# A sum and difference form for the last two inverse transforms, a third buffer for w2, and a new order from its first third on

## The chip, the cores and the metric

The kernel runs on one core of one Trainium2 chip. A core has five engines, each with a queue of its own that is worked off in order: TensorE (PE in the profile, with its weight loads as PEld) multiplies matrices into accumulators (PSUM), VectorE (DVE) and ScalarE (ACT) work element by element, GpSimd (POOL) does small set-up work and starts the accumulating and the scattering stores, and SyncE (SP) starts nearly all other transfers between HBM and the on-chip memory (SBUF). The metric is the device time of one execution in microseconds (us), as a median of runs.

## What is computed

The reference adds two branches under a gate. S is 2048 tokens, D 640 channels, F 1536.

```
x  = A_q                                            # (1, S, D), bf16
g  = sigmoid((x * gate_w).sum(-1))                  # one gate per token
# branch a: shift by 4 taps, long causal convolution over S, gate by q
kv = (sum over t<4 of k shifted by t * shift_k[:, t]) * v
y  = irfft(rfft(kv padded to 2S) * rfft(ssm_k padded to 2S))[:S]
a  = x * (y + kv * ssm_D)
# branch b: token-mixing MLP on the layer-normed x
u  = gelu(einsum("bsd,sf->bdf", layernorm(x), w1) + b1)
b  = einsum("bdf,fs->bsd", u, w2) + b2
out = g * a + (1 - g) * b
```

## The kernel before

**Branch a.** The 2048 tokens are cut into P = 4 blocks of 512. The convolution is done block by block in a frequency domain of 4 groups of 128 frequencies (`fi` 0 to 3): the filter's blocks go to tables `W0` to `W3`, the blocks j of kv to tiles `A0`, `A1` (a product with cosine and sine tables on TensorE, function `a_freq`), and VectorE forms the products `A[j] * W[m - j]` and adds them up for output block m in a tile `Z` (function `pair`; three real products stand for a complex one). Blocks 0 and 1 of kv are done early, blocks 2 and 3 late. Z of the last block is finished in four pieces, one a frequency group.

**The inverse.** `inverse(m_)` takes Z of output block m_ back to tokens. It makes four results of 128 x 640, P and Q for k = 0 and 1, each the sum of four products of a 128 x 128 table (`TIc`, `TIs` or a negated copy in `TIn`) with Z's four frequency groups. A product is two matmuls, because 640 columns are taken as two halves of 320. For the last block the products are issued frequency by frequency, for the others result by result. ScalarE copies the four results to a tile `pq` (evictions).

**The epilogue.** `epilogue(m_)` takes sums and differences of `pq` into `y` (VectorE), multiplies with `xe`, which is x times the gate, and adds to the output: blocks 0 to 2 by an accumulating store onto rows that the other branch has written, block 3 on chip, one token tile of 128 at a time, with stores of its own.

**Branch b.** After the layer norm, `mlp1` makes u in six steps, and `mlp2(q)`, q = 0 to 7, multiplies it with a block of w2 of 256 tokens (768 KB), loaded by `w2_load` to `w2_0` or `w2_1` in turn. A block is 2 token tiles of 12 products of two matmuls. For q of 6 and 7 ScalarE also makes a reversed copy `w2r` of half the block. The result of token tile 14 stays in its accumulator until VectorE adds it in the epilogue of block 3; its column halves are computed one after the other.

**The order.** Building the kernel first lists all operations (`_Plan.add`, numbered as they are created), with what each must wait for, worked out from the overlap of the memory that they touch. `_Plan.run` then issues them in the order of the list `ORDER`, which is written out in the file, and each engine's queue, SyncE's and GpSimd's included, has its operations in that order. Four accumulators of 128 x 1280 are handed out in turn as `ORDER` goes. The addresses of all SBUF tiles are written out in `OFFS`; tiles that are not needed at the same time share addresses. Matmuls are issued in line 311, ScalarE's operations in line 691, VectorE's two-operand ones (`tt`) in line 653, so the profile's groups are told apart by their tiles.

Of the kernel before, what the change touches and what calls it, by code (L numbers as in the profile page):

```python
# [422 lines left out]
def _checked(items, offs, base, top):  # L423
# [49 lines left out]
def _build(nc, A_q, A_k, A_v, A_shift_k, A_ssm_k, A_ssm_D, B_x, B_w1, B_b1, B_w2, B_b2, gate_w, out):  # L473
# [13 lines left out]
    FOLD = (2, 3)  # L487
    NSET = FT // FSET
# [3 lines left out]
    with ExitStack() as es:  # L492
# [62 lines left out]
        buf("TIn", [128, 4, 128], BF16, 45, END)  # L555
        buf("wz", [128, 128], BF16, 0, 8)
# [33 lines left out]
        for i in range(2):  # L590
            buf(f"w2_{i}", [128, FT, 256], BF16, 101, END)
        for i in range(2):
            buf(f"pq{i}", [128, 4, D], BF16, (64, 67)[i], END)
# [10 lines left out]
        for name, shape, dtype, t0, t1 in spec:  # L604
# [263 lines left out]
        iota(b["rev"][:, :], [[256, NT // 2]], 255, -1, 0.4)  # L868

# [341 lines left out]
        def w2_load(q):  # L1211
            nm = f"w2_{q % 2}"
            dma(b[nm][:, :, :], dram(B_w2, q * 256, [[S, 128], [128 * S, FT], [1, 256]]), nm, 40.0 + q)
# [4 lines left out]
        def mlp2(q):  # L1218
            plan.tag = f"m2_{q}"
            w2_load(q)  # L1220
            w2 = b[f"w2_{q % 2}"]
# [33 lines left out]
        def inverse(m_):  # L1255
# [7 lines left out]
            }  # L1263
            pq = b[f"pq{m_ % 2}"]
# [4 lines left out]
            last = m_ == P - 1  # L1269
            if last:  # L1270
                for k in range(2):
                    for fi in ORD:
                        mms = []
                        for w in "PQ":
                            c = 0 if w == "P" else 1
                            mms += halves(res[w, k], [(tabs[w, k][fi], Z[:, c, fi, :])], fi == 0, fi == 3)
                        pe([res["P", k], res["Q", k]], mms, 1.0)
            else:
# [8 lines left out]
            return pq  # L1287

        def epilogue(m_, pq, pr):
            y = b["y"]  # L1290
            t0 = 4 * m_
            o_ = b[f"o{m_ % NO}"]
            xe = b[f"xe{m_ % 2}"]
# [144 lines left out]
```

## Time and profile before

| what | value |
|---|---|
| median of three runs | 190.25 us (190.23, 190.25, 191.79) |
| the profiled execution | 190.98 us, span 189.2 us |
| TensorE busy | 178.8 us, 95% of the span, 1590 matmuls |
| VectorE busy | 175.5 us, 93%, 246 operations |
| ScalarE busy | 125.5 us, 66%, 202 operations |
| GpSimd busy | 35.2 us, 19% |
| transfers | 40.37 MB, mean 213 GB/s |

The span is the time from the first to the last instruction of the program in the profiled execution; what the execution takes beyond it lies around the program. Busy is the time in which an engine had at least one instruction under way. The rows of a time order show start, duration, engine, line, operation, the tile written, the tiles read, and in brackets the idle time before it with what ended it. Consecutive like instructions are merged (x and their count). A row of a group shows line, engine, operation, shapes, count, then busy time and mean duration in ns of one, then idle time before. Instructions of an engine overlap in the records: one starts before the one before it has been written out, so the distance between starts is shorter than a duration. A row by stretch shows the stretch, its length, the busy time and count of PE, PEld, DVE, ACT and POOL, the granted clock of TensorE, the share of the transfer engines and GB/s.

### The profile page before, as it was taken

To read this page: it belongs to the slowest core of one execution; us is meant where nothing else is said; L and a number is where in the kernel's file an instruction comes from. 1 tells how busy PE (TensorE), PEld (TensorE's weight loads), DVE (VectorE), ACT (ScalarE), POOL (GpSimd) and SP (SyncE) were. 2 spreads that over 40 slices of the span, in tenths; PEclk is the share of its full clock that TensorE was granted. 3 is DMA by queue.
4 is the path that set the end of the run, shared out by engine and by line. 5 is a ranking of instruction groups with operands and counts; after the bars stand their busy time and mean duration, and the time that the engine had idled before them with its cause. 6 is when DMAs were issued, how large, how long until landed. Compare 5 with 4: busy or idle time off the path is not lost.

```text
span 189.2 us, 3940 instructions
## 1 busy us (share of the span) xinstructions
PE 178.8 (95%) x1590; PEld 123.0 (65%) x1590; DVE 175.5 (93%) x246; ACT 125.5 (66%) x202; POOL 35.2 (19%) x68
## 2 busy tenths in 40 slices
PE   7778899999999999999999999999999899999992
PEld 2345666566667757777767777777667577777771
DVE  7999999999999999999899999999999999997352
ACT  4978999787699489439823047706778482495930
POOL 8366076610000000101000000000005003110732
PEclk9999999999999999999999999999999999999999
DMA  5999999798996876787948998997988976979992
GB/s 155 315 325 272 130 152 282 221 222 190 236 326 129 196 202 181 151 248 164 232 67 221 231 243 197 219 242 205 309 280 224 225 226 221 232 215 240 175 166 69
DMA packets 81094, 40.37 MB, mean 213 GB/s; under 512 B 40051, under 2 KB 80884, under 8 KB 81076
## 3 DMA queue, kind: packets, MB, share of 16 engines
q1 hardware_dynamic: 78340, 37.18, 78.5%
q0 software_dynamic: 2736, 2.95, 9.3%
q8 instruction: 12, 0.20, 0.4%
q14 instruction: 6, 0.05, 0.1%
HBM read 26.03 MB, written 7.54 MB: 177 GB/s over the span
## 4 chain that ended last, share of the span: by engine, by line
PE 61%; DVE 22%; ACT 4%; issue 4%; DMA 4%; POOL 2%; POOLq 1%; DVEq 0%
PE pp L311 61%; DVE stats L919 6%; DMA w<-in_B_w_dram 4%; DVE v L653 3%; DVE en L653 3%; DVE es L653 2%; DVE idx L660 2%; DVE W L653 2%; ACT pq L691 1%; POOL rstd L924 1%; ACT xe L691 1%; DVE h L661 1%; DVE eo L1006 1%; DVE mv L921 1%; DVE A L653 1%
## 5 line engine op out<-in xcount | busy, mean ns | idle before, releaser
L311 PE MATMUL pp<-h,w 128*128 128x320 bf16 x384 | 57.1, 299 | 0.2
L311 PE MATMUL pp<-gT,w 128*128 128x320 bf16 x336 | 48.4, 299 | 0.9 <-DMA w<-in_B_w_dram 0.9
L311 PEld LDWEIGHTS pp<-h,w 128*128 128x128 bf16 x384 | 36.8, 98 | 15.9 <-issue 1.8
L311 PEld LDWEIGHTS pp<-gT,w 128*128 128x128 bf16 x336 | 32.6, 98 | 14.0 <-DMA w<-in_B_w_dram 1.4
L653 DVE TENSOR_TENSOR tt<-A,W 128x3840 bf16<-128x3840 bf16 (+2 forms) x16 | 27.8, 1738 | 0.3
L691 ACT ACTIVATE A<-pp 128x640 bf16<-128x640 f32 x32 | 21.3, 700 | 9.3 <-PE pp L311 9.3
L653 DVE TENSOR_TENSOR Z<-Z,tt 128x3840 bf16<-128x3840 bf16 (+1 forms) x14 | 26.2, 1868 | 0.2
L262 POOL DMA_DIRECT2D out_dram<-xe x3 | 3.8, 1252 | 73.0 <-DVE Z L653 68.4
L691 ACT ACTIVATE o<-pp,c,omg 128x640 bf16<-128x640 f32 x13 | 11.2, 881 | 6.8 <-PE pp L311 6.4
L691 ACT ACTIVATE ks<-pp 128x512 bf16<-128x512 f32 (+1 forms) x24 | 11.1, 518 | 6.1 <-PE pp L311 6.1
L691 ACT ACTIVATE gT<-pp,bf 128x640 bf16<-128x640 f32 x12 | 9.4, 792 | 8.2 <-PE pp L311 8.1
L691 ACT ACTIVATE xe<-xe,gg 128x640 bf16<-128x640 bf16 x16 | 12.7, 827 | 2.4 <-DMA xe<-rows_q 1.2
L919 DVE BATCH_NORM_STATS2 stats<-x 128x6 f32<-128x320 bf16 x32 | 13.7, 472 | 0.0
L653 DVE TENSOR_TENSOR Z<-A,W 128x3840 bf16<-128x3840 bf16 x6 | 12.8, 2154 | 0.9 <-PE pp L311 0.8
L691 ACT ACTIVATE pq<-pp 128x640 bf16<-128x640 f32 x16 | 10.3, 702 | 4.8 <-PE pp L311 4.8
L671 POOL MEMSET W<- 1x640 bf16 x4 | 2.7, 665 | 50.9 <-ACT nq L691 49.6
L691 ACT ACTIVATE W<-pp 128x640 bf16<-128x640 f32 x18 | 12.0, 722 | 0.1
L653 DVE TENSOR_TENSOR W<-W 128x2560 bf16<-128x2560 bf16 x8 | 11.9, 1486 | 0.0
L653 DVE TENSOR_TENSOR y<-pq 128x1280 bf16<-128x1280 bf16 (+1 forms) x10 | 6.6, 688 | 4.5 <-ACT pq L691 4.5
L311 PE MATMUL pp<-kT,dg 64*64 64x256 bf16 x320 | 10.5, 271 | 0.3 <-ACT Wo L691 0.3
L311 PE MATMUL pp<-eo,TFc 128*128 128x320 bf16 x48 | 8.9, 300 | 1.1 <-ACT TFc L691 1.1
L653 DVE TENSOR_TENSOR Z<-Z 128x1280 bf16<-128x1280 bf16 (+1 forms) x16 | 9.9, 653 | 0.1
(147 smaller groups left out, 303.6 us busy)
## 6 DMA issues: line engine op xcount, KB each, us to landing
w<-in_B_w_dram SPq DMA_DIRECT2D x24, 256.0 KB, 4.1
w<-in_B_w_dram SPq DMA_DIRECT2D x8, 768.0 KB, 5.1
wnat<-in_A_ssm_k_dram SPq DMA_DIRECT2D x4, 640.0 KB, 5.7
x<-in_A_q_dram SPq DMA_DIRECT2D x7, 320.0 KB, 6.3
out_dram<-o SPq DMA_DIRECT2D x6, 320.0 KB, 6.1
v<-in_A_v_dram SPq DMA_DIRECT2D x4, 320.0 KB, 4.5
rows_q<-in_A_q_dram SPq DMA_DIRECT2D x8, 160.0 KB, 3.2
xe<-in_A_q_dram SPq DMA_DIRECT2D x4, 320.0 KB, 5.8
```

What stands on the lines that cost most here:

```text
L262: ins = engobj.dma_start(out_ap, in_ap, accum_op=ALU.add)
L311: ins = self.nc.tensor.matmul(ps_ap, lhsT=lhsT, rhs=rhs, start=start, stop=stop)
L653: return vop(eng, c, lambda e: e.tensor_tensor(out_, in0, in1, op), [in0, in1], [out_], pr, kind="tt")
L660: return e.tensor_scalar(out_, in0, s1, None, op0=op0)
L661: return e.tensor_scalar(out_, in0, s1, s2, op0=op0, op1=op1)
L671: return vop(eng, 0.03 + nel(ap) / 1200.0, lambda e: e.memset(ap, val), [], [ap], pr, kind="ms")
L691: return e.activation(out_, src, func, **kw)
L919: vop("DVE", 0.393, (lambda o_, i_: lambda e: e.bn_stats(o_, i_))(o_, i_), [i_], [o_], pr, kind="bn")
L921: vop("DVE", 0.11, (lambda o_, i_: lambda e: e.bn_aggr(o_, i_))(o_, i_), [i_], [o_], pr, kind="ba")
L924: vop("POOL", 0.7, (lambda o_, i_, e_: lambda e: e.tensor_tensor(o_, i_, e_, ALU.pow))(b["rstd"][:, sl], b["vpe"][:, sl], bc(c_mh, [[8, 12 ...
L1006: vop("DVE", 0.74, lambda e: e.tensor_copy(dst, src()), [src], [dst], 0.3, ps=[p_], kind="ev")
```

## The change

Three things are changed.

1. For blocks 2 and 3 (`UV`), the inverse makes other results. The tables are such that, for k = 0 and k = 1, frequency groups 0 and 1 enter a pair of results with different tables, while groups 2 and 3 enter with the same table up to a sign. A new table `TU` (six parts of 128 x 128) holds half the sum and half the difference of `TIc` and `TIs` for two of the four groups, and a negated copy. With it the four results are the half-sum and half-difference of the former P's and of the former Q's, and in each of the four one product is empty (`None`): three products stay of four. After the evictions VectorE takes the sum and the difference of these, for P and Q at once (two `tt` over 2 x 640 elements a partition), into `y`; these are the former four results. `epilogue` then works with `pq` and `y` exchanged. `TU` is made by two `tt` on VectorE and two scalings on ScalarE (`tu_make`).
2. w2 gets a third buffer, `w2_2`, at an address that a tile of w1 and one of kv's tiles used before; the blocks q = 0 to 7 go to buffers 0, 1, 0, 1, 2, 0, 1, 2.
3. `ORDER` is new from its entry 404 on. Operations created behind `tu_make` have numbers 4 higher, those behind inverse(2) 6 and those behind inverse(3) 8 higher, so the entries before that differ in the list are in part the same operations. Among other things the new order puts block 3's kv products on VectorE earlier, the loads of w2's blocks 4 to 7 earlier, the first tile of w2's block 6 ahead of inverse(3), the four evictions of inverse(3) ahead of the last reversed copy of w2, and the products of token tile 15 ahead of all but the first of tile 14's.

```
@@ ORDER: 861 entries for 853 @@
...
-    384, 377, 400, 274, 407, 540, 385, 361, 401, 417, 542, 541, 436, 544, 273, 435, 282, 359, 448, 437, 360, 546, 449, 416,
+    385, 377, 545, 553, 384, 281, 400, 359, 282, 544, 401, 361, 546, 436, 435, 547, 416, 437, 548, 274, 407, 555, 454, 438,
...
+    UV = (2, 3)
...
+        buf("TU", [128, 6, 128], BF16, 101, END)
...
+        buf("w2_2", [128, FT, 256], BF16, 120, END)
...
-            "ncol": 211776, "A0": 211840, "TIs": 227200, "b2x": 228224, "wz": 228288, "gz": 228544,
+            "ncol": 211776, "A0": 211840, "TIs": 227200, "b2x": 228224, "TU": 100224, "w2_2": 182912, "wz": 228288, "gz": 228544,
...
+        def tu_make():
+            plan.tag = "tu"
+            TU = b["TU"]
+            tt(TU[:, 0:2, :], TIc[:, 2:4, :], TIs[:, 2:4, :], ALU.add, 30.0)
+            tt(TU[:, 2:4, :], TIc[:, 2:4, :], TIs[:, 2:4, :], ALU.subtract, 30.0)
+            act(TU[:, 0:4, :], TU[:, 0:4, :], ACT.Copy, 30.0, scale=0.5)
+            act(TU[:, 4:6, :], TU[:, 2:4, :], ACT.Copy, 30.0, scale=-1.0)
...
-            nm = f"w2_{q % 2}"
+            nm = f"w2_{(0, 1, 0, 1, 2, 0, 1, 2)[q]}"
...
+            if m_ in UV:
+                TU = b["TU"]
+                tabs = {
+                    ("P", 0): [TU[:, 0, :], TU[:, 3, :], None, ti(TIc, 3)],
+                    ("Q", 0): [TU[:, 0, :], TU[:, 5, :], ti(TIs, 2), None],
+                    ("P", 1): [TU[:, 2, :], TU[:, 1, :], ti(TIc, 2), None],
+                    ("Q", 1): [TU[:, 4, :], TU[:, 1, :], None, ti(TIs, 3)],
+                }
...
+            for k in range(2):
+                fis = {w: [fi for fi in ORD if tabs[w, k][fi] is not None] for w in "PQ"}
+                def part(w, sel):
+                    c = 0 if w == "P" else 1
+                    return halves(res[w, k], [(tabs[w, k][fi], Z[:, c, fi, :]) for fi in sel],
+                                  sel[0] == fis[w][0], sel[-1] == fis[w][-1])
+                if m_ == P - 1:
                     for fi in ORD:
+                        ws = [w for w in "PQ" if fi in fis[w]]
+                        pe([res[w, k] for w in ws], [m for w in ws for m in part(w, [fi])], 1.0)
+                else:
                     for w in "PQ":
+                        pe([res[w, k]], part(w, fis[w]), 1.0)
...
-            return pq
+            if m_ not in UV:
+                return pq, b["y"]
+            y = b["y"]
+            tt(y[:, 0:3:2, :], pq[:, 0:3:2, :], pq[:, 1:4:2, :], ALU.add, 50.0)
+            tt(y[:, 1:4:2, :], pq[:, 0:3:2, :], pq[:, 1:4:2, :], ALU.subtract, 50.0)
+            return y, pq
...
         def epilogue(m_, pq, pr):
-            y = b["y"]
+            pq, y = pq
...
+        tu_make()
         kv_two(2)
```

More of the change, by code (lines that the diff above doesn't have):

```diff
@@ L1220, in mlp2 @@
             w2_load(q)
-            w2 = b[f"w2_{q % 2}"]
+            w2 = b[f"w2_{(0, 1, 0, 1, 2, 0, 1, 2)[q]}"]
             o_ = b[f"o{(q // 2) % NO}"]
@@ L1268, in inverse @@
                     res[w, k] = _PS()
-            last = m_ == P - 1
-            if last:
-                for k in range(2):
-                    for fi in ORD:
[L1273 to L1278, printed above, removed]
-                for k in range(2):
+            for k in range(2):
[5 more added lines that the diff above has]
+                if m_ == P - 1:
+                    for fi in ORD:
+                        ws = [w for w in "PQ" if fi in fis[w]]
+                        pe([res[w, k] for w in ws], [m for w in ws for m in part(w, [fi])], 1.0)
+                else:
                     for w in "PQ":
-                        c = 0 if w == "P" else 1
-                        pe([res[w, k]], halves(res[w, k], [(tabs[w, k][fi], Z[:, c, fi, :]) for fi in ORD]), 1.0)
+                        pe([res[w, k]], part(w, fis[w]), 1.0)
             for k in range(2):
```

42 rows, old and new, of the table ORDER are left out of this document.

## The prediction

> **What bounds the kernel now.** I read the page's shares and its chain of waits first, then that chain in order of time, then the engines by stage.
>
> ```profile
> span 189.2 us, 3940 instructions
> PE 178.8 (95%) x1590; PEld 123.0 (65%) x1590; DVE 175.5 (93%) x246; ACT 125.5 (66%) x202; POOL 35.2 (19%) x68
> PE 61%; DVE 22%; ACT 4%; issue 4%; DMA 4%; POOL 2%; POOLq 1%; DVEq 0%
> ```
> ```profile
> 49.74 92.22 PE pp L311 x858
> 141.96 6.96 DMA w<-in_B_w_dram
> ```
> ```profile
> 100.00:142.00 42.00, 42.00 (x413) 30.43 (x402) 41.65 (x31) 21.51 (x39) 0.00 (x0) 1.00 0.96 238
> 149.00:170.00 21.00, 21.00 (x155) 15.08 (x156) 20.57 (x26) 12.02 (x17) 2.58 (x3) 1.00 0.85 215
> 170.00:185.60 15.60, 15.54 (x115) 10.96 (x112) 8.46 (x16) 9.66 (x13) 5.54 (x6) 1.00 0.87 181
> ```
>
> TensorE holds most of the chain (61%): it carries it alone from 49.74 for 92 us. Its busy time equals the stretch in the first two rows and misses it by 0.06 in the third, and the granted clock is 1.00 in each. The one hole is the weight tile `w` of the second token matmul. VectorE is just as full, but only up to 170: in 170 to 185.6 it is busy for 8.46 us of 15.6. ScalarE has room everywhere. So two engines stand side by side until Z of the last block is done, and then TensorE alone has work that waits for nobody: the second token matmul. The matmuls of the last stage, in order of time:
>
> ```profile
> 146.82 1.25 PE L311 MATMUL pp<-gT,w 128*128 128x320 bf16 x8
> 148.96 2.35 PE L311 MATMUL pp<-gT,w 128*128 128x320 bf16 x16 [0.89 <-DMA w<-in_B_w_dram]
> 154.95 9.94 PE L311 MATMUL pp<-gT,w 128*128 128x320 bf16 x72
> 183.75 1.79 PE L311 MATMUL pp<-gT,w 128*128 128x320 bf16 x12
> ```
>
> The hole is 0.89 us. The 72 matmuls take 9.94 us, and a matmul by itself 0.30 (the 299 ns of the groups below), so one comes every 9.64/71 = 0.136 us. The last ends at 183.75 + 1.79 = 185.54. VectorE's end, and what follows it:
>
> ```profile
> 167.72 2.09 DVE L653 TENSOR_TENSOR Z<-Z 128x640 bf16<-128x640 bf16 x5
> 170.43 1.56 DVE L653 TENSOR_TENSOR y<-pq 128x1280 bf16<-128x1280 bf16 x2 [0.62 <-ACT pq L691]
> 173.87 0.49 DVE L653 TENSOR_TENSOR y<-pq 128x640 bf16<-128x640 bf16 x1 [0.35 <-ACT pq L691]
> 177.92 1.29 DVE L653 TENSOR_TENSOR y<-pq 128x640 bf16<-128x640 bf16 x3 [3.56 <-ACT pq L691]
> 184.87 0.49 DVE L653 TENSOR_TENSOR xe<-xe,o 128x640 bf16<-128x640 bf16 x1 [2.52 <-ACT o L691]
> 185.27 1.01 DVE L1327 SCALAR_TENSOR_TENSOR xe<-pp,omg,xe 128x320 bf16<-128x320 f32 x2
> ```
> ```profile
> 176.58 1.30 ACT L691 ACTIVATE pq<-pp 128x640 bf16<-128x640 f32 x2
> 183.95 0.88 ACT L691 ACTIVATE o<-pp,c2x,omx 128x640 bf16<-128x640 f32 x1 [2.92 <-PE pp L311]
> 182.37 4.31 SPq L265 DMA_DIRECT2D out_dram<-xe  x3
> ```
>
> Z of block 3 is whole at 169.81. After that VectorE waits for ScalarE's evictions four times. The last two operations, which add the matmul result of token tile 14, end at 186.28; the last store is issued up to 186.68, and the span ends at 189.2, so 2.92 us lie behind VectorE's last operation. The profiled execution took 190.98, which is 1.78 more than its span; the median of the three runs is 190.25. I work against the span and take the difference off the median, since two of the three runs are at 190.23 and 190.25.
>
> **The change, part by part.**
>
> *Fewer matmuls.* Blocks 2 and 3 have four results each, each a sum of four products; of every result one product goes. Two column halves make that 4 x 2 = 8 matmuls a block.
>
> ```profile
> L311 PE MATMUL pp<-Z,TIs 128*128 128x320 bf16 x36 | 7.3, 299 | 0.0
> L311 PE MATMUL pp<-Z,TIc 128*128 128x320 bf16 x36 | 7.2, 299 | 0.0
> L311 PE MATMUL pp<-Z,TIn 128*128 128x320 bf16 x24 | 5.4, 299 | 0.0
> ```
>
> These rows are the inverse of blocks 1 to 3: 96 matmuls, 32 a block, so 24 stay in each of two. Sixteen at 0.136 us are 2.18 us, on an engine without holes. Their weight loads (98 ns each) run beside matmuls and add nothing. The Trainium skill, page "TensorE: Matmul & The Clock Gate", section "Back-to-back issue gap", speaks against the size of this: it gives 81 ns a matmul at 128 columns and 131 at 512 in a stream of loads and matmuls, by which 320 columns would be near 106 ns (an estimate between its two figures), sixteen of them 1.7 us, and the forecast 0.5 us later. The trace's 136 ns decides.
>
> *The third w2 buffer.* Today the load of w2's block 4 goes to the buffer of block 2 and cannot start before that is read.
>
> ```profile
> 141.96 0.60 SPq L265 DMA_DIRECT2D w<-in_B_w_dram  x1
> DMA to landing us min/median/max: 3.2/5.0/7.0
> ```
>
> It is issued at 141.96 and lands 6.96 us later (the chain's row), the longest of the tile's 3.2 to 7.0. In the new list it stands at place 649 instead of 686, behind block 2's load and six loads of `xe`. Block 2's load waits for block 0's last product, which by the new order ends near 127; seven issues of 0.4 to 1.2 us put block 4's at about 132, landing by 139 even with 7 us. Its first matmul moves forward too: 296 matmuls from there to the end are 40.2 us, so it comes about 142.3. The margin is 3 us, and the 0.89 us go. Blocks 5 to 7 get their buffers earlier for the same reason.
>
> *What VectorE gets.* Four passes over 1,280 elements (sum and difference, two blocks) and two of 256 for the table `TU`.
>
> ```profile
> 130.26 0.82 DVE L653 TENSOR_TENSOR y<-pq 128x1280 bf16<-128x1280 bf16 x1
> 131.00 2.15 DVE L653 TENSOR_TENSOR tt<-A,W 128x3840 bf16<-128x3840 bf16 x1
> L653 DVE TENSOR_TENSOR v<-es 128x1280 bf16<-128x1280 bf16 x8 | 6.4, 818 | 0.0
> L653 DVE TENSOR_TENSOR c<-omg,bf 128x16 f32<-128x16 f32 x1 | 0.2, 167 | 0.0
> ```
>
> A pass of 1,280 starts 0.74 us before the next operation. The new ones take every second row of a tile; half of the passes `v<-es` read so too, and last 0.82 like the others. Writing every second row is not shown; split into two passes of 640 (0.49 us each with 0.08 overlapped, the row at 173.87) one would cost 0.82, so it is 0.74 to 0.82, and I take 0.74: four are 2.96 us. A 256-element pass lies between 0.17 (16 elements, the last row) and 0.49 (640); I take 0.2, two make 0.4. In all 3.36 us on the full engine. What of it counts: the table's 0.4 us falls ahead of Z3's end. The first difference of block 2 is queued ahead of the last subtraction of Z3, another 0.74. All of Z3 but that subtraction (0.41) is then ready at 169.81 + 0.4 - 0.41 = 169.8, and its last piece at 169.81 + 0.4 + 0.74 = 170.95. By the new order the earliest matmul that reads a piece made just before 169.8 has 88 matmuls from itself to the end, and the one that reads the last piece has 66; counted back from a TensorE end of 182.5 they start at 170.5 and 173.5. The margins are 0.7 and 2.5 us, and the second token matmul covers the rest. If that cover went, each microsecond past the margin would be one on the end.
>
> *ScalarE* gets two scalings of the table, 512 and 256 elements.
>
> ```profile
> L691 ACT ACTIVATE TIn<-TIs 128x128 bf16<-128x128 bf16 x2 | 0.7, 332 | 0.0
> L691 ACT ACTIVATE w2r<-w 128x1536 bf16<-128x1536 bf16 x2 | 3.0, 1479 | 0.0
> 128.59 0.17 ACT L691 ACTIVATE gth<-pp 128x4 f32<-128x4 f32 x1 [5.62 <-PE pp L311]
> ```
>
> Between 0.33 us (128 elements) and 1.48 (1,536), a straight line gives 0.64 and 0.44, together 1.1. They are queued just after the row at 128.59, ahead of which ScalarE is idle for 5.62 us; inverse(2), which reads the table, comes after the hole at 148.96. Nothing of it counts.
>
> *The tail.* Here a wait is added: the first sum of block 3 reads all four evicted results, where today the pair of k = 1 is enough, and behind it stand every epilogue operation of block 3 and the stores. In exchange the four evictions now stand ahead of the 1.49 us reversal of w2 on ScalarE. The last matmul of inverse(3) has 64 behind it: 182.5 - 8.7 = 173.8. Two evictions lead to 175 at most; sum and difference end at 176.5, eight operations of 0.41 us at 179.8. Then comes the row of tile 15 (today's 184.87), which waits for its eviction: the matmuls of tile 15 end with 20 behind them, 182.5 - 2.7 = 179.75, and today 0.96 us pass from their end (183.91, which is 185.54 less twelve pitches) to 184.87. So it starts at 180.7, with VectorE 0.9 us early. Four operations of 0.41 and the last two (1.01) end at 183.35. From TensorE's side, today's 0.74 us between its end and VectorE's (186.28 - 185.54) give 183.2. Both agree, against 186.28 today.
>
> *The sum.* -2.18 - 0.89 = -3.07 on TensorE (end 182.47), -2.93 at VectorE's last operation, and the same 2.92 behind it: span 186.27, which is 187.3 against the median. Adding up each engine's new order with the starts and durations of the trace, I find about twenty places where ScalarE hands an accumulator to TensorE with less than 0.5 us to spare (nearest at about 117 us). Today such a place looks like this:
>
> ```profile
> 132.03 6.71 PE L311 MATMUL pp<-gT,w 128*128 128x320 bf16 x48
> 138.68 0.30 PE L311 MATMUL pp<-es,AFs 128*128 128x320 bf16 x1
> ```
>
> The last of the 48 starts at 138.44, the next matmul 0.24 later instead of 0.136: 0.10 us lost. I count six of these after 60 us, 0.6 us in all. The new order may lose less (down to none, 0.6 us gained) or more (1 us, if half of the twenty do). I add 0.2: **187.5 us**.
>
> **Rivals.**
>
> *VectorE becomes the bound.* Its margin at Z3 is 0.7 us.
>
> ```profile
> 136.12 1.55 DVE L653 TENSOR_TENSOR v<-kt,v 128x1280 bf16<-128x1280 bf16 x2
> 119.38 3.38 SPq L260 DMA_TRANSPOSE xt<-in_A_q_dram  x1
> v<-in_A_v_dram SPq DMA_DIRECT2D x4, 320.0 KB, 4.5
> ```
>
> The first product of block 3's `v` moves from 136.12 to about 128.4, and its load, behind the transposed load of the second row, which comes a microsecond later, is issued at about 123.5: with the 4.5 us of the last row it lands at 128. For it: no margin there, and a load may take 7 us, as one of `w` did; VectorE is then 2 us late and TensorE 1.3: 188.8. Against: 4.5 is the median of four. It gives 188.0 to 189.3.
>
> *The third buffer does not take the wait away,* or another of its size appears at an earlier `w`: 0.89 back, 188.4. Against it stands the 3 us of margin.
>
> *The transfers back up (slower).* The new list issues from 123.4 to about 133.5 what today is spread up to 142: three blocks of w2 (768 KB), three loads of 320 KB and six of 160, 4.3 MB up to and with w2's block 3, whose first matmul comes at about 143.
>
> ```profile
> 123.00:141.00 18.00, 18.00 (x152) 12.98 (x150) 17.83 (x15) 9.56 (x17) 0.00 (x0) 1.00 1.01 270
> 125.00:130.00 5.00, 5.00 (x55) 3.74 (x54) 4.93 (x3) 1.29 (x4) 0.00 (x0) 1.00 0.79 168
> ```
>
> Today this stretch moves 270 GB/s with the engines' share at 1.01, full. At that rate 4.3 MB take 16 us, landing at 139.4. At 220 GB/s the margin is gone; at 190 the wait is 3 us and the gain is used up (190.3). At the 168 of the second row it is 25.8 us and a wait of 6.2: 193.4. So it decides from 220 GB/s down, and is slower than before below 190. Against it: the low row is a lull with a share of 0.79, not a limit.
>
> *The new order eats the gain* in small waits: the lists agree up to entry 404 of 853, and twenty handovers losing 0.15 us each cost 3 us: 190.3. Against it: today's list has been full over the same stretch, and shows one hole.
>
> **How the numbers follow.** The forecast has 0.62 (187.2 to 187.9). VectorE as the bound 0.13, the wait that stays 0.08, the small waits 0.08, the backed-up transfers 0.09. About 1% either way, 188.35 and 192.15, is what a measurement of this kernel can tell, its three runs being 0.8% apart. Faster by more: the forecast, half of VectorE's case and half of the wait that stays, 0.72. Slower: the transfers' case and 0.01 of the small waits, 0.10. Within: the rest, 0.18. The range goes from 186.6 (today's 0.6 us of late matmuls gone as well, from 187.3) to 189.9, which leaves out the transfers' case and the small waits.
>
> **What would show it.** TensorE: 80 matmuls on `Z`, 8 fewer from each of blocks 2 and 3, its last ending near 182.5, and no hole at a `w` load. The load of block 4 issued near 132. VectorE: four more passes `y<-pq` of 1,280 elements near 0.74 us, and its last operation near 183.35. The store rows as today, 2.9 us behind it. I am wrong if TensorE shows holes after 60 us of over 1 us in sum: ended by `Z` or `es`, VectorE is the bound; by `w`, the transfers; by ScalarE's evictions, the order. If TensorE ends at 182.5 and the span does not follow, the tail's sum was wrong.

## The result

| | before | after |
|---|---|---|
| median of 6 runs each, taken together | 191.05 us (190.23 to 191.88) | 188.41 us (187.38 to 188.71) |
| profiled execution, its span | 190.98, 189.2 | 188.71, 186.9 |

The ratio is **0.9862, with a 95% interval of 0.9827 to 0.9896**: faster by 1.4%. The forecast was 187.5 us for a kernel at 190.25, a ratio of 0.986. The kernel before itself has medians between 190.25 and 191.05 from one set of runs to the next, so only ratios are compared below.

The page of the changed kernel, its size, its engines and the shares of the chain:

```profile
span 186.9 us, 3913 instructions
PE 175.8 (94%) x1574; PEld 121.6 (65%) x1574; DVE 178.9 (96%) x252; ACT 126.9 (68%) x204; POOL 35.3 (19%) x68
PE 56%; DVE 27%; DMA 8%; issue 2%; POOL 2%; SPq 1%; ACT 1%; DVEq 0%; POOLq 0%
```

The lines are those of the changed file, three further on than before (L653 is L656, L691 is L694). VectorE is now busier than TensorE (178.9 against 175.8 us), and 8% of the chain are transfers, where it was 4%. The chain in order of time names two of them:

```profile
102.39 4.41 DMA w<-in_B_w_dram
...
133.57 10.38 DMA w<-in_B_w_dram
144.00 36.61 PE pp L311 x268
```

Two loads of `w`, one of them 10.38 us from its issue to its landing; after it TensorE carries the chain alone. The busy times by stage (stretch, its length, PE, PEld, DVE, ACT, POOL, then clock, DMA share and GB/s):

```profile
100.00:142.00 42.00, 41.69 (x434) 30.32 (x432) 41.61 (x33) 22.96 (x43) 0.00 (x0) 1.00 1.03 241
142.00:149.00 7.00, 6.32 (x47) 4.36 (x46) 7.00 (x10) 4.98 (x8) 2.38 (x2) 1.00 0.98 286
149.00:170.00 21.00, 21.00 (x157) 15.11 (x156) 20.79 (x23) 13.38 (x17) 4.00 (x4) 1.00 1.01 219
170.00:183.00 13.00, 13.00 (x97) 9.24 (x96) 10.70 (x20) 9.38 (x12) 4.86 (x5) 1.00 0.77 158
```

TensorE is full from 149 to the end, as it was; it misses 0.31 us before 142 and 0.68 in 142 to 149. Its matmuls around these places, and the last ones:

```profile
106.85 3.43 PE L311 MATMUL pp<-h,w 128*128 128x320 bf16 x24 [0.19 <-DMA w<-in_B_w_dram]
...
142.07 1.25 PE L311 MATMUL pp<-gT,w 128*128 128x320 bf16 x8
144.00 1.26 PE L311 MATMUL pp<-gT,w 128*128 128x320 bf16 x8 [0.68 <-DMA w<-in_B_w_dram]
...
180.43 2.88 PE L311 MATMUL pp<-gT,w 128*128 128x320 bf16 x20
```

The hole of 0.89 us at a `w` load is gone from where it was, and 0.68 + 0.19 us stand at two other `w` loads. TensorE ends at 180.43 + 2.88 = 183.31 instead of 185.54. VectorE's operations in the tail:

```profile
175.72 1.56 DVE L656 TENSOR_TENSOR y<-pq 128x1280 bf16<-128x1280 bf16 x2 [1.25 <-ACT pq L694]
...
181.55 0.49 DVE L656 TENSOR_TENSOR xe<-xe,o 128x640 bf16<-128x640 bf16 x1 [0.81 <-ACT o L694]
...
182.89 0.57 DVE L663 TENSOR_SCALAR xe<-xe,c 128x640 bf16<-128x640 bf16 x1
183.57 1.01 DVE L1352 SCALAR_TENSOR_TENSOR xe<-pp,omg,xe 128x320 bf16<-128x320 f32 x2
```

VectorE ends at 184.58, 1.27 us behind TensorE (0.74 before). The account of the span, before to after, 189.2 to 186.9:

- sixteen matmuls fewer: -2.18 on TensorE;
- waits at `w`: 0.89 gone, 0.87 come: -0.02, and 0.03 of small handovers; TensorE's end moves by -2.23;
- VectorE's distance to TensorE's end: +0.53;
- what lies behind VectorE's last operation: 2.32 instead of 2.92, -0.60.

That is -2.30. The matmuls gave nearly all of it. The third buffer gave nothing that this execution shows.

### The profile page after: what moved, and what is told of

Same layout as the page of the kernel before. It is cut to its first block, busy times and chain, and to the rows that moved or that the text cites. A ratio compares the mean times of both kernels' runs of the same rounds, so it can differ in the third digit from the quotient of the medians.

```text
span 186.9 us, 3913 instructions
## 1 busy us (share of the span) xinstructions
PE 175.8 (94%) x1574; PEld 121.6 (65%) x1574; DVE 178.9 (96%) x252; ACT 126.9 (68%) x204; POOL 35.3 (19%) x68
## 4 chain that ended last, share of the span: by engine, by line
PE 56%; DVE 27%; DMA 8%; issue 2%; POOL 2%; SPq 1%; ACT 1%; DVEq 0%; POOLq 0%
PE pp L311 56%; DMA w<-in_B_w_dram 8%; DVE stats L930 6%; DVE v L656 3%; DVE en L656 3%; DVE Z L656 2%; DVE W L656 2%; DVE idx L663 2%; DVE es L656 2%; POOL rstd L935 1%; DVE tt L656 1%; DVE h L664 1%; SPq L265 1%; DVE eo L1017 1%; DVE mv L932 1%
## 5 line engine op out<-in xcount | busy, mean ns | idle before, releaser
L656 DVE TENSOR_TENSOR tt<-A,W 128x3840 bf16<-128x3840 bf16 (+2 forms) x16 | 27.8, 1738 | 0.2
L694 ACT ACTIVATE A<-pp 128x640 bf16<-128x640 f32 x32 | 21.3, 702 | 8.1 <-PE pp L311 8.1
L656 DVE TENSOR_TENSOR Z<-Z,tt 128x3840 bf16<-128x3840 bf16 (+1 forms) x14 | 26.1, 1867 | 0.1
L694 ACT ACTIVATE pq<-pp 128x640 bf16<-128x640 f32 x16 | 11.0, 703 | 7.2 <-PE pp L311 7.1
L694 ACT ACTIVATE gT<-pp,bf 128x640 bf16<-128x640 f32 x12 | 9.5, 790 | 8.3 <-PE pp L311 8.3
L694 ACT ACTIVATE xe<-xe,gg 128x640 bf16<-128x640 bf16 x16 | 12.8, 827 | 1.8 <-DMA xe<-rows_q 1.7
L694 ACT ACTIVATE o<-pp,c,omg 128x640 bf16<-128x640 f32 x13 | 11.4, 880 | 3.7 <-PE pp L311 3.7
L694 ACT ACTIVATE ks<-pp 128x512 bf16<-128x512 f32 (+1 forms) x24 | 11.3, 523 | 3.1 <-PE pp L311 3.1
L656 DVE TENSOR_TENSOR Z<-A,W 128x3840 bf16<-128x3840 bf16 x6 | 12.8, 2154 | 0.5 <-PE pp L311 0.5
L694 ACT ACTIVATE W<-pp 128x640 bf16<-128x640 f32 x18 | 12.1, 719 | 1.5 <-PE pp L311 1.5
L656 DVE TENSOR_TENSOR W<-W 128x2560 bf16<-128x2560 bf16 x8 | 11.9, 1487 | 0.2
L656 DVE TENSOR_TENSOR Z<-Z 128x1280 bf16<-128x1280 bf16 (+1 forms) x16 | 10.0, 654 | 0.1
L262 POOL DMA_DIRECT2D out_dram<-rows_o x6 | 7.0, 1396 | 14.9 <-DMA out_dram<-o 14.0
```

The costliest lines, as they stand in the source:

```text
L262: ins = engobj.dma_start(out_ap, in_ap, accum_op=ALU.add)
L656: return vop(eng, c, lambda e: e.tensor_tensor(out_, in0, in1, op), [in0, in1], [out_], pr, kind="tt")
L694: return e.activation(out_, src, func, **kw)
```

## The experiments

Each ratio is to the kernel before, run together with it. Waits of TensorE, matmul ends and landing times are those of one profiled execution.

**Sixteen matmuls put back.** The change, but one product of each of the eight results is added twice:

```diff
-  [(tabs[w, k][fi], Z[:, c, fi, :]) for fi in sel]
+  [(tabs[w, k][fi], Z[:, c, fi, :]) for fi in sel
+   for _ in range(2 if m_ in UV and fi > 1 else 1)]
```

> The changed kernel with the sixteen matmuls put back: in blocks 2 and 3 each result adds one of its three products twice, from the same table and the same piece of Z, so that no new wait arises (the results of these blocks differ for it). All else, the passes of VectorE, the third buffer and the order, is that of the change. If TensorE sets the end and a matmul costs 0.136 us there, the sixteen cost 2.18 us: TensorE's last matmul ends near 185.5 instead of 183.31, and the time is 2.2 us over that of the change, a ratio to the kernel before of about 0.998. If VectorE had become a bound beside it, part of the sixteen would lie beside its work: less than 1.5 us over the change, a ratio under 0.994.

Measured: 0.9996 (0.9963 to 1.0029). TensorE's last matmuls, and its waits at `w` (sum, times, longest):

```profile
182.21 2.88 PE L311 MATMUL pp<-gT,w 128*128 128x320 bf16 x20
```
```profile
PE pp L311 <- DMA w<-in_B_w_dram: 0.5, 2, 0.3
```

TensorE ends at 185.09, 1.78 us later than in the change, with 0.5 us of waits at `w` instead of 0.9: the sixteen cost 2.2 us, 0.137 each, and take the whole gain with them. With them in, the new order, the third buffer and the VectorE passes together stand where the kernel before stood. No run has the new order without the new inverse; this one comes nearest to it.

**The third buffer alone, in the old order.** The load of w2's block 4 goes to a third buffer and is issued sooner:

```diff
-  nm = f"w2_{q % 2}"
+  nm = f"w2_{(0, 1, 0, 1, 2, 0, 1, 2)[q]}"
   ...
   SyncE's part of ORDER (734 is the load of block 4):
-  709, 721, 683, 719, 673, 695, 697, 734
+  709, 721, 683, 719, 734, 673, 695, 697
```

> The kernel before with nothing but the third buffer for w2: the load of block 4 goes to it and stands in the list right behind the load of xe that was issued at 135.16, instead of at 141.96. If the wait for the buffer is the cause of the hole, the load is issued near 136.5, lands before 147 and the 0.89 us at the w load go: a span of 188.3, a ratio of 0.995. If the transfers are backed up, the load takes 10 us and more from its issue, lands at 147 to 148, and part of the hole stays, or transfers behind it come late: a ratio of 0.998 to 1.00.

Measured: 1.0003 (0.9971 to 1.0036), no gain. In the trace the load is issued at 137.78 and lands at 145.60, TensorE does not wait for it, and no gap of more than 0.12 us is left behind 115 us. But TensorE had waited earlier, for other transfers (0.4 us for a `w` at 38 us beside this row):

```profile
PE pp L311 <- DMA kT<-in_A_k_dram: 1.4, 1, 1.4
```

A second execution of the same kernel was profiled, to tell whether that wait belongs to it.

> The kernel before with the third buffer alone, a second look. In the first profile the hole at the w load was gone, but TensorE had waited 1.4 us for the transposed load of kT near 20 us, which the kernel before had not (its load landed 12.4 us from its issue, here 14.4). If that wait is a matter of how fast the transfers go in one execution, it is smaller or gone here and the span is near 188.1; if it belongs to this kernel, it is there again at 1 us or more, and the span is near 189.5. The hole at w is gone in both cases.

```profile
PE pp L311 <- DMA kT<-in_A_k_dram: 0.8, 1, 0.8
```
```profile
143.15 0.44 PE L311 MATMUL pp<-v,AFs 128*128 128x320 bf16 x2 [0.38 <-ACT A L692]
```

It took 191.14 us, span 189.3. The wait, which stands near 30 us in both traces and not near 20, is 0.8 us here (with 0.9 for a `w` at 35), the hole at block 4's load is gone again, and 0.38 us of TensorE are lost at 143.15 to ScalarE instead. From 52 us on both traces show the saving: the product of `en` with `TFc` that starts at 51.91 in the kernel before starts 1.43 and 0.67 us later here, TensorE's last matmul ends only 0.36 and 0.16 us later, so 1.07 and 0.51 us are gained in between. The transfers ahead of 52 us took as much or more. A wait for `kT` is in a trace with two buffers too (0.5 us in a run below) and is missing in several with three, so I take these waits for a property of the execution.

The buffer alone still brings no time that can be measured: the lowest of its twelve runs is 190.13 us, the lowest of 28 of the kernel before 189.93. Nor has the hole one size: counted from start to start, less the usual 0.136, TensorE loses 1.05 us at block 4's load in the kernel before (0.89 of them idle), but 0.25 and 0.12 us in the traces of the next two runs, which have two buffers as well. Why the median does not fall by 0.9 us stays open.

**The inverse alone, in the old order with two buffers.** The new operations are set into the old list, each right behind what it reads.

> The old order and two buffers with the new inverse of blocks 2 and 3 alone: the table's four operations and the four sums and differences are set into the old list, each right behind what it reads, and the operations of block 3 that were ahead of its sum are moved behind it. If the sixteen matmuls are the gain, 2.18 us go and the hole of 0.89 us at the w load stays: a span of 187.0, a ratio of 0.989. If VectorE becomes the bound it is less: in the old order the first matmul of inverse(3) starts 1.55 us behind the end of the piece of Z that it reads (168.61 to 170.16), eight matmuls of inverse(2) lie ahead of it (1.09 us) and two table passes of about 0.25 us come ahead of the piece, so that the margin is used up almost exactly; with each further 0.1 us on VectorE the saving would shrink by as much, and a ratio over 0.993 would say so.

Measured: **1.0132** (1.0085 to 1.0180): slower than before, which neither theory said. TensorE does end sooner, at 183.87 instead of 185.54; the span is 190.8. The loss is in the tail, and not at Z. SyncE's queue, ScalarE's wait, GpSimd's stores and VectorE's last operations there:

```profile
175.27 0.55 SPq L265 DMA_DIRECT2D rows_o<-xe  x1
175.91 0.56 SPq L265 DMA_DIRECT2D xe<-rows_q  x1
176.52 0.61 SPq L265 DMA_DIRECT2D rows_o<-xe  x1
```
```profile
180.47 1.55 ACT L693 ACTIVATE xe<-xe,gg 128x640 bf16<-128x640 bf16 x2 [3.27 <-DMA xe<-rows_q]
```
```profile
182.34 1.81 POOL L262 DMA_DIRECT2D out_dram<-rows_o  x2 [4.63 <-DMA rows_o<-xe]
184.46 1.25 POOL L730 DMA_INDIRECT out_dram<-xe,rev  x1 [0.30 <-DVE xe L655]
186.01 1.01 POOL L730 DMA_INDIRECT out_dram<-xe,rev  x1 [0.30 <-DVE xe L1351]
```
```profile
184.65 1.00 DVE L1351 SCALAR_TENSOR_TENSOR xe<-pp,omg,xe 128x320 bf16<-128x320 f32 x2
```

VectorE has block 2's result at 175.24 instead of 173.52, since the sum and difference (1.56 us) come ahead of it. Block 2's row store in SyncE's queue therefore goes out 1.72 us later, at 175.27, and the load of `xe` for block 3, whose buffer had been free for 7 us (the last store out of it, issued at 165.71, landed at 168.77), stands behind it, beside two additions of GpSimd that start at 175.53 and 176.27. It lands 4.54 us later, ScalarE waits 3.27 us, and VectorE ends 1.78 us behind TensorE. GpSimd's additions wait 4.63 us for the second row store, its last stores go out behind them, and 5.2 us lie behind VectorE's end. One edit tests the first link:

```diff
   SyncE's part of ORDER (836 is the load of xe, 779 and 781 the row stores):
-  747, 779, 836, 781
+  747, 836, 779, 781
```

> The old order with the new inverse alone, as in the run before (ratio 1.013), and one edit: the load of xe that stood behind the first row store of block 2 in SP's queue goes ahead of it, behind the store that was issued at 167.78. In that run the store was issued at 175.27, the load behind it at 175.91, it landed 4.54 us later, ScalarE waited 3.27 us for it and VectorE's last operations followed. If that wait is the cause of the loss, it goes, VectorE ends near 184.5 instead of 185.65, and the span falls to 188.5 to 189.3: a ratio of 0.998 to 1.003. What is then left is the row stores of block 2 and the additions that GpSimd issues for them, which start 1.7 us later than in the kernel before (VectorE is that much later at block 2's results) and crowd the end. If the loss were TensorE's waits instead, nothing would change: 1.013.

Measured: 0.9993 (0.9966 to 1.0020), as expected; 2.7 us come back.

```profile
169.59 0.53 SPq L265 DMA_DIRECT2D xe<-rows_q  x1
176.16 1.21 SPq L265 DMA_DIRECT2D rows_o<-xe  x2
```

The load goes out at 169.59, ScalarE's wait is gone and VectorE ends at 185.50, 0.73 us behind TensorE. But TensorE ends at 184.77, not 183.4. It waited 0.6 us for the reversed copy of w2 that ScalarE makes for the matmuls behind inverse(2), 0.4 us at a load of `w` at 113.57, and ahead of 52 us 0.9 us at another `w` and 0.5 us for `kT`, of which 0.40 us are left at 52. In the change's trace no matmul waits for that copy.

**Both in the old order,** without and with that edit:

> The old order with both, the new inverse as in the run without the buffer and the third buffer as in the run with it alone. If the two savings add up, 2.18 + 0.89 = 3.07 us go: a span of 186.1, a ratio of 0.984. If VectorE is what comes next in the old order, the matmul that reads the first whole piece of Z of block 3 now wants it 0.9 us earlier than VectorE has it, and TensorE waits there for what it saved at the w load: a span near 187.0, a ratio of 0.989, and a wait of 0.5 to 1 us of TensorE for Z in the trace. I hold the second likelier, 0.6 to 0.4.

Measured: 1.0093 (1.0055 to 1.0130). Both expectations missed, for the reason just shown (ScalarE waits 3.19 us for the same load of `xe`); TensorE did not wait for Z at all, so my fear for that piece was unfounded.

> The old order with everything of the change but its order: the new inverse, the third buffer, and the one edit that mended the run of the inverse alone, the load of xe ahead of block 2's row store (ratio 0.999 without the buffer). In that run TensorE waited 0.12 us in all at the one place near 150 us that was a hole of 1.05 us in the kernel before, so if the buffer is worth what TensorE loses at w, it brings next to nothing: a ratio of 0.996 to 1.000, and the rest down to 0.986 is the new order's. If the buffer frees 0.9 us wherever it stands: 0.9945 or less.

Measured: 0.9950 (0.9927 to 0.9973), 0.4% better than the same without the buffer; a hole of 0.9 us would be 0.5%. The two intervals overlap by a hair, and the trace without the buffer lost only 0.12 us at that load, so the buffer's worth is between nothing and the full hole. From here to the change's 0.986 it is the new order, since the two kernels differ in nothing else. Where it gains is shown in part: in this run too TensorE waited 0.6 us for the reversed copy, and it ended at 184.49 (0.88 us of that lost ahead of 52 us) with 0.74 us more up to VectorE's end.

**The late load in the new order.** The third buffer is given to w2's block 3, whose load was the late one, instead of block 4:

```diff
-  (0, 1, 0, 1, 2, 0, 1, 2)[q]
+  (0, 1, 0, 2, 1, 0, 2, 1)[q]
   ...
   SyncE's part of ORDER: 738 (block 4) and 713 (block 3) change places
   TensorE's part (743, 744 block 4; 714, 715 block 3):
-  743, 714, 656, 744, 660, 715
+  714, 656, 715, 743, 744, 660
```

> The changed kernel with the third buffer given to block 3 of w2 instead of block 4: block 3's load takes the place in the list that block 4's had and no longer waits for block 1's last product, block 4's takes the later place, and the first three groups of matmuls of the two blocks change places, block 3's first. In the changed kernel block 3's load was issued at 133.57, the moment block 1's last product ended (133.54), landed 10.38 us later behind 3.5 MB of other loads, and TensorE waited 0.68 us for it. If the place in the queue is the cause, block 3's load lands before 142.1, block 4's near 144 with its first matmul at 144.7, both waits go, TensorE ends 0.7 to 0.8 us earlier, and the span is near 186.1: a ratio to the kernel before of 0.982. If a load of that size cannot land sooner there whatever its place, or if VectorE is as close behind as TensorE, the wait shows up at block 4's load or at a piece of Z, and the time stays: 0.986.

Measured: 0.9845 (0.9812 to 0.9878), as expected in the trace: no wait at `w` behind 60 us, and

```profile
179.20 2.88 PE L311 MATMUL pp<-gT,w 128*128 128x320 bf16 x20
```

TensorE ends at 182.08, and the span is 185.5. Block 3's load landed at 140.93 for a first matmul at 141.69, block 4's at 143.18 for one at 144.14. In time the step of 0.2% is inside the intervals. The same four loads in four executions that have the old assignment (the change, the sixteen put back, the tail's run, two passes more), by the view of the tile `w` from 120 to 150 us; the last number is that of block 3:

```profile
DMA to landing us min/median/max: 5.5/7.8/10.4
```
```profile
DMA to landing us min/median/max: 5.4/7.9/9.8
```
```profile
DMA to landing us min/median/max: 4.9/6.8/9.2
```
```profile
DMA to landing us min/median/max: 5.7/8.4/11.0
```

The waits at block 3 are 0.68, none, none and 1.0 us. So the hole is there or not with a few per cent in the speed of the transfers, and its size in the profiled execution of the change is one draw.

**VectorE's last operations.** The change with two operations moved ahead of the row that waits:

```diff
   VectorE's part of ORDER (856 is the row of tile 15, 858 the product of tile 12, 845 the bias of tile 14):
-  844, 856, 858, 859, 845, 846, 848
+  844, 858, 845, 856, 859, 846, 848
```

> The changed kernel with two of VectorE's last operations moved: the product of tile 12 and the addition of the bias of tile 14 go ahead of the row of tile 15, which waits 0.81 us for ScalarE's eviction; they ran behind it. If VectorE's own order sets the end, that wait is filled, its last operation ends near 183.9 instead of 184.58 (0.6 us behind TensorE instead of 1.27), and the span falls by 0.6 us: a ratio of 0.983. If the end is set by TensorE's last matmul and the stores alone, nothing changes: 0.986.

Measured: 0.9855 (0.9819 to 0.9890).

```profile
181.50 0.54 DVE L1352 SCALAR_TENSOR_TENSOR xe<-pp,omg,xe 128x320 bf16<-128x320 f32 x1
182.49 0.55 DVE L1352 SCALAR_TENSOR_TENSOR xe<-pp,omg,xe 128x320 bf16<-128x320 f32 x1 [0.44 <-PE pp L311]
```

The last operation now waits for TensorE's last matmul (0.44 us), as it should, and ends 0.59 us behind it instead of 1.27. In the trace the step is right; in time it cannot be told from the change. This execution had no wait at a `w`, and TensorE ended at 182.45, where the prediction had put it (182.47).

**VectorE's margin.** Two, and then six, further passes of 1,280 elements ahead of the last pieces of Z of block 3:

```diff
+  if m_ == 2:
+      for _ in range(2):      # 6 in the other
+          tt(y[:, 0:2, :], b["Z0"][:, 1, 0:2, :], b["Z0"][:, 1, 2:4, :], ALU.add, 50.0)
```

> The changed kernel with two more passes of 1,280 elements on VectorE, 1.48 us, ahead of the last four pieces of Z of block 3 and of the sum and difference of block 2 (their result is overwritten). If VectorE has the margin that the trace of the change shows (piece ended 169.40, read 171.18, a margin of 1.78 us; the next 3.65 us), TensorE does not wait; the store of block 2 and the sums of block 3 come at most 0.25 us later, since VectorE stood idle for 1.25 us ahead of these: a time within 0.3 us of the change, a ratio of 0.986 to 0.988. If VectorE has become the bound, all 1.48 us are on the end: 0.994.

Measured: 0.9909 (0.9870 to 0.9948), which reaches from the one expectation to the other. In the trace TensorE waited for no piece of Z, only for `w`:

```profile
PE pp L311 <- DMA w<-in_B_w_dram: 1.3, 3, 1.0
```

Its last matmul ends at 183.68, 0.37 later than in the change, with 0.27 us more of such waits behind 60 us (the third wait, 0.19 us at 44.80, is made up by 52), and VectorE 1.08 us behind. The two passes take 1.59 us from the first's start to what follows them, and not 1.48. So in this execution they cost TensorE 0.1 us at most; what the median shows over the change is not explained by it.

> The changed kernel with six more passes of 1,280 elements on VectorE, 4.44 us, at the place where two cost TensorE no wait. The margin at the first piece behind them was 1.78 us, so if VectorE has just that margin TensorE waits 2.6 to 2.7 us for Z at inverse(3), its last matmul and the end come later by as much, 190.3 to 191.2 us in all: a ratio of 0.997 to 1.003. If VectorE were the bound already, all 4.44 us are on the end: 1.009; if there is more room than the margin says, the ratio stays under 0.993.

Measured: 1.0144 (1.0082 to 1.0206), more than expected. The profiled execution is the longest of its four (197.02 us against 192.57 to 194.81), so its sizes are not those of the ratio. What TensorE waited for, and then its busy time in stretches around the wait (columns as above; the clock is the number behind POOL):

```profile
PE pp L311 <- DVE Z L657: 3.8, 1, 3.8
```
```profile
160.00:172.90 12.90, 12.90 (x96) 9.09 (x93) 12.69 (x19) 9.43 (x13) 4.00 (x4) 1.00 1.09 242
172.90:176.70 3.80, 0.02 (x1) 0.00 (x0) 3.70 (x6) 0.57 (x1) 0.00 (x0) 0.85 0.41 139
177.20:182.40 5.20, 5.20 (x21) 2.99 (x20) 4.39 (x6) 1.41 (x2) 0.37 (x1) 0.50 0.00 0
182.40:191.70 9.30, 9.23 (x68) 6.38 (x66) 6.76 (x14) 6.47 (x8) 4.78 (x5) 1.00 0.74 123
```

The wait for Z is there, so VectorE's margin is finite; it is not the bound of the change. The six passes take 5.03 us (168.77 to 173.80), 0.84 each and not 0.74, which is part of the reason why the loss is more than expected; the margin lies between the 1.59 us of the two passes and these 5.03. And the wait costs a second time: behind 3.8 us of idleness the granted clock is 0.50 from 176.7 to 182.4, and the matmuls start 0.267 us apart there (eight from 177.23 to 179.37) instead of 0.136. The four executions have mean clocks of 0.983, 0.997, 0.990 and 0.982 at 197.02, 192.57, 193.31 and 194.81 us, so the slower ones seem to share it; that is read off four numbers and not shown.

**All three edits together:** block 3 in the third buffer, VectorE's last operations, and

```diff
   SyncE's part of ORDER (583, 584 loads of w1; 503, 505 loads of v):
-  503, 584, 505, 583
+  503, 584, 583, 505
```

> The changed kernel with the third buffer given to block 3, VectorE's last operations in the order of the tail run, and the first of the two late w1 loads (issued at 102.39 in the change, its matmul waited 0.19 us) put ahead of a load of v that is needed 1.3 us later. If the w loads and the tail are separate, they add: TensorE without a hole after 90 us ends near 182.0 (182.08 in the run with the buffer changed), VectorE 0.6 us behind it, and with 2.35 us behind that the span is 184.9: a time of 186.7, a ratio of 0.980. If the tail's saving was only that its profiled execution had no wait at w, the end stays where that of the buffer run was: a span of 185.5, a ratio of 0.9845.

Measured: 0.9817 (0.9779 to 0.9856), 187.40 us, the lowest of all kernels here, though its interval overlaps that of the change.

```profile
PE pp L311 <- DMA kT<-in_A_k_dram: 1.5, 1, 1.5
```
```profile
182.95 0.55 DVE L1352 SCALAR_TENSOR_TENSOR xe<-pp,omg,xe 128x320 bf16<-128x320 f32 x1 [0.44 <-PE pp L311]
```

The profiled execution lost time to `kT` and, 0.3 us, to a `w` at the start (its matmuls near 70 us run 0.83 us behind those of the buffer's run); TensorE ends at 182.91, which is 182.08 without that, VectorE 0.59 us later, and the span is 185.9. The span of 184.9 that I expected is 185.1 without that loss, and the best two of the six runs have it.

## Why the prediction came out right, and where its steps did not

**Fewer matmuls: right.** 2.18 us was the term, 2.2 us is what the sixteen cost when put back. The Trainium skill, page "TensorE: Matmul & The Clock Gate", section "Back-to-back issue gap", gives sustained figures by which I had estimated 106 ns at 320 columns; the runs show 0.136 us. The same section's formula for an isolated matmul at the full clock, N/2.4 + 2.5 ns, gives 135.8 ns at 320, and that is what this stream runs at: here the trace agrees with the formula and not with the sustained figures.

**The third buffer: the step that failed.** "The margin is 3 us, and the 0.89 us go." Block 4's load was issued where I said (131.81, against "about 132") but landed at 141.73 and not by 139: the margin was 0.3 us. Behind it block 3's load, which I had not followed in this part, waited for its buffer until block 1's last product ended (133.54), was issued at 133.57 and landed at 143.96. Its 0.68 us and 0.19 at a w1 load took the place of the 0.89. That was the rival "the transfers back up", in a size between its cases. The rate was right, the amount was not:

```profile
124.00:133.00 9.00, 9.00 (x86) 6.75 (x85) 8.97 (x10) 3.71 (x9) 0.00 (x0) 1.00 0.97 254
133.00:144.00 11.00, 10.32 (x76) 7.22 (x75) 10.90 (x9) 10.23 (x19) 0.00 (x0) 1.00 1.10 285
```

These two make 271 GB/s, my 270; but 5.4 MB moved in these 20 us, where I had counted 4.3 MB up to block 3's load. I had started from an empty queue: a transposed load issued at 121.01 was still landing until 126.30, and stores issued from 135.73 (the first landed at 144.75) were under way beside the loads ahead of them.

**VectorE's passes: right, in the new order.** The groups by shape (busy us, mean ns):

```profile
L656 DVE TENSOR_TENSOR y<-pq 128x1280 bf16<-128x1280 bf16 x8 | 6.5, 820 | 1.3 <-ACT pq L694 1.3
...
L694 ACT ACTIVATE TU<-TU 128x512 bf16<-128x512 bf16 x1 | 0.6, 615 | 0.0
L656 DVE TENSOR_TENSOR TU<-TIc,TIs 128x256 bf16<-128x256 bf16 x2 | 0.6, 288 | 0.0
L694 ACT ACTIVATE TU<-TU 128x256 bf16<-128x256 bf16 x1 | 0.4, 405 | 0.0
```

Passes that write every second row take 0.82 us, 0.74 with the overlap, as those that only read so. The table's passes took 0.29 each where I took 0.2, ScalarE's scalings 0.62 and 0.41 (0.64 and 0.44). The two pieces of Z that I named ended at 169.40 and 170.54 (169.8 and 170.95 forecast), with 1.78 and 3.65 us to spare; since TensorE came 0.84 us later than forecast, that is 0.9 and 2.8 beside the 0.7 and 2.5. The rival of VectorE as the bound did not come; the run with six passes shows that it can. That the passes are hidden is the order's doing: in the old one they delay block 2's store and the load behind it, and the kernel is slower than before until that load is moved.

**The tail: two errors that cancel.** The row of tile 15 began at 181.55, which is the forecast's 180.7 and TensorE's 0.84. From there VectorE took 3.03 us and not 2.65: the addition of the bias and what follows it start 0.68 us apart (182.89 to 183.57) instead of 0.41, and another start is 0.11 late. I had let the order stand although VectorE is idle for 0.81 us just ahead. Behind VectorE's end I had kept 2.92 us; it is 2.32, and 2.3 to 2.4 in every trace of the new order. Before, GpSimd's last store went out beside SyncE's last two; now it is 2 us ahead of them (182.32 against 184.15 and 184.61):

```profile
185.64 1.01 POOL L728 DMA_INDIRECT out_dram<-xe,rev  x1 [3.53 <-DVE xe L653]
```
```profile
182.32 1.01 POOL L731 DMA_INDIRECT out_dram<-xe,rev  x1 [0.59 <-DVE xe L656]
```

That this is what shortens the end is not shown by a run of its own.

**The sum.** The forecast's span was 186.47 (186.27 and 0.2 in reserve), the profiled execution's is 186.9: 0.84 us of TensorE that did not go, 0.39 more in the tail, 0.60 less behind it, and the reserve of 0.20 that was not needed. That execution is the longest of its six, 0.3 us over their median, so the medians' ratio comes out at the forecast's 0.986. In part this is luck. As a time the forecast was 0.9 us too low (187.5 against 188.41); the ratio agrees because the kernel before came out 0.8 us higher beside it (191.05) than the 190.25 that I started from. And the steps did not each hold: the hole stayed, and the tail's two errors offset each other and more. In the two executions of the new order without a wait at a `w` or for `kT`, TensorE ended at 182.45 (the tail's run) and 182.08 (the buffer's), 0.02 and 0.39 us ahead of the forecast's 182.47.

## What to carry to other kernels

Count the work that leaves a full engine by its pitch there: that term held (2.2 us for 2.18), and the rest of the change was about not losing it again. When a load is pulled forward, follow the one that stands behind it, and start the count of bytes from what is still landing and not from an empty queue. A load queued behind a store waits for that store's producer, so time on an engine with room can cost more than itself at the end (here 1.7 us on VectorE and 2.7 us of the whole).

## What the runs showed that I had not expected

- **A wait costs twice.** 3.8 us without matmuls brought the granted clock to 0.50, and 5.7 us of matmuls passed before it was 1.00 again. The Trainium skill, page "TensorE: Matmul & The Clock Gate", section "What's actually happening", gives an idle window of about 3.4 us for the fall and as long a busy one for the return. The trace differs on both: the clock is 1.00 up to 175.5 and 0.50 from 176.0, and the mean of 0.85 over the 3.8 us puts the fall 2.7 us behind the last matmul; the return took 5.7.
- **Executions differ by their transfers.** In two kernels whose lists differ only in operations issued behind 100 us, the transposed loads of `kT` at the start took 10.0 us at most from issue to landing in one run (first line, the tail's) and 14.4 in another (second line, the last one); TensorE waits for them from about 13.5 on.

```profile
DMA to landing us min/median/max: 9.1/9.6/10.0
```
```profile
DMA to landing us min/median/max: 14.4/14.4/14.4
```

- **In every trace here the loads of SyncE's queue land in the order of their issue**, so that one of 768 KB, which took 4.5 us where the queue was short (`w` in the kernel before, issued at 115.64), took 10.38 behind 2.9 MB of loads issued since 127.28 (3.7 MB with itself, where an expectation above says 3.5).
